# Attention and a gated long convolution on one core: the written order of all steps laid out anew, the last output rows staged in the buffers of k and v, the second sum on GpSimd in some batches

## The chip, the cores and the metric

The kernel runs on one core of a Trainium2 chip. The metric is the time of one execution on the device in microseconds (us). The engines are TensorE (PE; its weight loads are PEld), VectorE (DVE), ScalarE (ACT), GpSimd (POOL) and SyncE (SP). Each works through its own instructions in the order in which the program wrote them, and waits on semaphores for the others. SP, ACT and POOL also start transfers (DMAs).

## What is computed

Eight batches, each with 8 heads, 576 positions and 64 values a head. A linear attention without softmax is normalised and handed, as 576 x 512, to a gated convolution over the positions:

```python
def _attn_ref(q, k, v, g_norm):
    kv = np.einsum('bhsd,bhse->bhde', k, v)
    out = np.einsum('bhsd,bhde->bhse', q, kv)
    rms = np.sqrt(np.mean(out * out, axis=-1, keepdims=True) + 1e-06)
    return out / rms * g_norm
...
    x = attn_out.transpose(0, 2, 1, 3).reshape(B, S, H * D)
    proj = x @ w_proj
    x1, x2, x3 = proj[..., :D], proj[..., D:2 * D], proj[..., 2 * D:]
    X2 = np.fft.rfft(x2, n=S, axis=1)
    H = np.fft.rfft(filter_fft, n=S, axis=0)
    x2_conv = np.fft.irfft(X2 * H, n=S, axis=1)
    return (x1 * x2_conv * x3) @ w_out
```

Inputs and output are float32; products run in bfloat16.

## The kernel before, in words

The Fourier transforms are matmuls with tables of sines and cosines (IV, and FW, FX, FY, FT, FZ made from it by transposes), cut into three parts by folding the positions first (even and odd halves, then thirds). Everything is written as small steps, one function each in the dictionary `step`; the string `ORDER` names them one by one with their batch ("M0.3" is step M0 of batch 3), and a loop at the end calls them in that order. No scheduler moves anything: the string is the order of every engine's queue. A third number ("T0.0.18") puts so many idle matmuls (line 110, of zeros) in front of the step. PSUM is four pairs of banks; `take` hands a step the pair that has been free longest, and the step that evicts it calls `free`, so the order also decides who waits for whose eviction.

The steps of a batch, by engine:

- Loads on POOL's queue: Lk, Lv, Lq (a, b: half the heads), into two buffers each of k, v and q. Once at the start: the tables (Zi, Z, Zd, Zt, An, Zf, Tb0 to Tb2), the filter Lf with its products Ff (line 313) and H (lines 330, 333), and the weights Lw1 (first gate), Lw2 (x2), Lw3 (third), Lwo.
- q turned: T0, T1 on TensorE with the copies eTa, eTv (batches 0 and 1, line 413), Qt by transfers on SP, with a small copy on POOL that waits for it (line 401), from batch 2 on.
- K (line 375) multiplies k and v, eK (line 381) casts the product; O01 and O23 (line 440) multiply with q; sq (line 450, ACT) squares, R (line 447, PE) sums the squares, rs (line 461, ACT) takes the inverse root; ob (ACT, line 457) or ov (DVE, line 455) scales by g_norm; x0, x1 (DVE, line 475; two heads' pairs each) make x.
- eo, fr, fa (DVE, lines 487 to 498) fold x; rrM, rrT, abM, abT (PE, lines 515 to 535) multiply it with the middle third of w_proj; err, eab, eT (ACT, line 539) cast that; F0, F1t, F1, F2c, F2 (PE, lines 552 to 579) transform it.
- M0, M1 (DVE, line 587) multiply by the filter's spectrum into tpw, M2 (line 602) the third part; A0 and A1 are the sums of these products on POOL, Av0 and Av1 the same on DVE (all line 593). Before, A0 and Av1 are used in every batch.
- I01, I23, Io01, Io23 (PE, lines 641, 642) transform back, and need all sums; ea, oa (ACT, line 645) cast; vB, w, fin (DVE, lines 651 to 663) unfold and multiply with the gates' product, into yg.
- Ga0 to Ga3 and Gb0 to Gb3 (PE, line 612) are the gates, 8 matmuls each; x10 to x13 (ACT, line 618) cast the first, g0 to g3 (DVE, line 620) multiply the second with it.
- U0, U2, U4 (PE, lines 696, 709) multiply yg with w_out; ot0, ot2, ot4 (ACT) copy the result into one of five buffers ot and issue four transfers on SP (lines 700 to 716). For batch 7, V0 to V3 (line 732) take 128 rows each, va, vv copy them (ACT, DVE; line 737) into an ot too, and ds, dg, da (line 742) send them 32 rows at a time from SP, POOL or ACT.

The start (batch 0 up to K.1) and the end (from M0.7 on) are where one batch stands alone; in between, steps of up to four batches are mixed.

Of the kernel before, what the change touches and what calls it, by code (L numbers as in the profile page):

```python
# [23 lines left out]
ob1.1 Lk.2 err.0 sq0.1 abM.0 Gb2.0 ob0.1 F0.0 g2.0 eab.0 abT.0 eT.0 O23.1 F2c.0 F2.0 M0.0 sq2.1 ob2.1 Gb1.0 F1t.0 F1.0
M2.0 sq3.1 HN1.0 ob3.1 R1.1 g1.0 Lq.2 R0.1 Ga3.0 rs1.1 rs0.1 R2.1 K.2 Lq.3 A0.0 Qt.2 M1.0 R3.1 Qt.3 x13.0 rs2.1 x0.1
rs3.1 eK.2 Lk.3 Lv.3 Gb3.0 Av1.0 Io01.0 oa01.0 I01.0 x1.1 O01.2 Lwo.0 g3.0 ea01.0 Ga1.1 eo.1 sq1.2 Io23.0 ob1.2 R1.2
x11.1 Lv.4 Ga0.1 rs1.2 I23.0 oa23.0 fa.1 abM.1 sq0.2 fr.1 x10.1 ob0.2 ea23.0 vB.0 w.0 eab.1 abT.1 O23.2 rrM.1 eT.1
sq3.2 R0.2 rrT.1 ob3.2 rs0.2 fin.0 F2c.1 F2.1 err.1 Gb1.1 sq2.2 F0.1 M2.1 Ga3.1 ob2.2 Lk.4 g1.1 R3.2 Lq.5 x13.1 Lq.4
F1t.1 F1.1 rs3.2 M0.1 K.3 eK.3 R2.2 M1.1 Gb3.1 rs2.2 Gb0.1 g3.1 O23.3 U0.0 sq2.3 sq3.3 x1.2 g0.1 Ga2.1 Av1.1 x0.2 A0.1
ob3.3 ot0.0 Io01.1 x12.1 eo.2 oa01.1 fa.2 Gb2.1 I01.1 Io23.1 ob2.3 ea01.1 g2.1 Lv.5 abM.2 I23.1 oa23.1 abT.2 ea23.1  # L30
eab.2 eT.2 Ga0.2 x10.2 O01.3 K.4 Ga1.2 Qt.4 sq0.3 fr.2 ob0.3 eK.4 sq1.3 rrM.2 x11.2 F1t.2 F1.2 vB.1 w.1 rrT.2 R2.3
ob1.3 err.2 Gb0.2 rs2.3 fin.1 M1.2 F0.2 U2.0 R3.3 g0.2 rs3.3 Gb1.2 M0.2 F2c.2 F2.2 A0.2 ot2.0 g1.2 R0.3 M2.2 R1.3
Ga2.2 rs1.3 Ga3.2 x1.3 rs0.3 x0.3 x12.2 O23.4 Lq.6 x13.2 sq2.4 Av1.2 Gb2.2 ob2.4 U4.1 Lk.5 sq3.4 eo.3 ob3.4 g2.2 ot4.1
U0.1 fa.3 fr.3 Qt.5 R3.4 Io01.2 ot0.1 oa01.2 abT.3 rs3.4 I01.2 eT.3 ea01.2 Gb3.2 Io23.2 g3.2 oa23.2 I23.2 abM.3 ea23.2
eab.3 O01.4 rrM.3 F1t.3 F1.3 sq0.4 vB.2 w.2 ob0.4 sq1.4 rrT.3 err.3 M1.3 U2.1 ob1.4 F0.3 Ga1.3 R1.4 fin.2 ot2.1 x11.3
Ga0.3 Gb0.3 M0.3 R0.4 A0.3 rs1.4 x10.3 Av1.3 F2c.3 F2.3 Lv.6 rs0.4 g0.3 Gb1.3 R2.4 M2.3 rs2.4 g1.3 Lk.6 K.5 Io01.3
I01.3 x1.4 oa01.3 x0.4 eK.5 Ga2.3 x12.3 ea01.3 Ga3.3 O23.5 Io23.3 x13.3 oa23.3 sq3.5 ob3.5 U0.2 ot0.2 eo.4 I23.3 sq2.5
ob2.5 fa.4 Gb2.3 ea23.3 Lk.7 g2.3 abM.4 O01.5 fr.4 eab.4 abT.4 Gb3.3 Qt.6 sq0.5 eT.4 ob0.5 sq1.5 rrM.4 g3.3 R3.5 rrT.4
rs3.5 err.4 K.6 F1t.4 F1.4 eK.6 Ga1.4 ob1.5 R0.5 Ga0.4 x11.4 vB.3 w.3 F0.4 rs0.5 x10.4 fin.3 M1.4 M0.4 F2c.4 F2.4 R1.5
U2.2 rs1.5 Gb1.4 R2.5 M2.4 ot2.2 A0.4 g1.4 Ga3.4 O23.6 rs2.5 x13.4 sq2.6 x1.5 Av1.4 ob2.6 Gb0.4 sq3.6 Gb3.4 ob3.6 g0.4  # L40
g3.4 Ga2.4 x12.4 U4.3 x0.5 O01.6 Io01.4 eo.5 ot4.3 sq0.6 U0.3 oa01.4 ob0.6 fr.5 sq1.6 I01.4 Gb2.4 ob1.6 ea01.4 Lq.7
rrM.5 Io23.4 Lv.7 ot0.3 R0.6 g2.4 I23.4 rrT.5 oa23.4 rs0.6 K.7 fa.5 ea23.4 R1.6 abT.5 err.5 abM.5 rs1.6 vB.4 w.4 R3.6
Qt.7 eT.5 eK.7 eab.5 F0.5 Ga1.5 rs3.6 R2.6 F1t.5 F1.5 x11.5 fin.4 F2c.5 F2.5 rs2.6 M0.5 U2.3 M1.5 A0.5 ot2.3 Ga0.5
x10.5 M2.5 Gb1.5 x1.6 g1.5 Av1.5 O23.7 sq2.7 Gb0.5 Ga2.5 ob2.7 sq3.7 g0.5 Ga3.5 x0.6 x12.5 ob3.7 eo.6 I01.5 fa.6 Gb2.5
Io01.5 x13.5 g2.5 U0.4 Io23.5 oa01.5 Ga0.6 ea01.5 ot0.4 fr.6 oa23.5 I23.5 abM.6 ea23.5 abT.6 x10.6 Gb3.5 eab.6 O01.7
eT.6 Ga1.6 vB.5 w.5 g3.5 sq1.7 F1t.6 F1.6 ob1.7 fin.5 x11.6 sq0.7 rrM.6 R0.7 rrT.6 ob0.7 rs0.7 M1.6 F2c.6 F2.6 R1.7
err.6 M2.6 Gb0.6 rs1.7 F0.6 g0.6 U0.5 R2.7 M0.6 Ga2.6 x0.7 rs2.7 R3.7 x12.6 Gb1.6 Gb2.6 A0.6 ot0.5 rs3.7 Av1.6 g1.6
Ga3.6 g2.6 Io01.6 x1.7 eo.7 fr.7 I01.6 x13.6 Gb3.6 oa01.6 g3.6 Io23.6 ea01.6 U2.4 ot2.4 rrM.7 fa.7 Ga0.7 I23.6 oa23.6
# [4 lines left out]
dg13.7 V2.7 vv2.7 da20.7 dg21.7 ds22.7 da23.7 V3.7 va3.7 ds30.7 dg31.7 da32.7 ds33.7 ot2.6"""


@with_exitstack
def kernel(
# [402 lines left out]
    def e_rs(b, j):  # L460
        act.activation(out=halves(rstd()[:, j]), in_=tmp['r', b, j][:, :, 0:TH], func=AF.Abs_reciprocal_sqrt, scale=1.0 / D, bias=bias_eps)  # L461
# [151 lines left out]

    def gate_ev(b, dc, part):
        pp = tmp['g', b, dc, part]
        x1 = buf("x1", dc % 2, [P, 2, TH])
        if part == 0:
            act.copy(out=x1, in_=pp[:, :, 0:TH])  # L618
        else:
            vec.tensor_mul(out=halves(g13t()[:, dc]), in0=pp[:, :, 0:TH], in1=x1)  # L620
# [76 lines left out]

    def U_ev(b, c0):
        ot = ot_tile()
        act.copy(out=ot, in_=tmp['u', b, c0])  # L700
        free(("u", b, c0))
        for i in range(4):
            nc.sync.dma_start(out=o_rows(b, 2 * (b % 2) + 4 * c0 + i, 2 * (b % 2) + 4 * c0 + 4 + i), in_=ot[32 * i:32 * i + 32])
# [30 lines left out]
    def V_ev(b, key, ev):  # L734
        ot = tmp['ot', b, key] = ot_tile()
        k_ = ("u4", b) if key == 4 else ("v", b, key)
        ev(out=ot[:, 0], in_=tmp[k_])
        free(k_)

    def V_out(b, key, i, q):  # L740
        rows = o_rows(b - 1 + i // 2, (NB - 2, NB - 1, 0, 1)[i]) if key == 4 else o_rows(b, 2 * (b % 2) + 4 * key + i)
        q.dma_start(out=rows, in_=tmp['ot', b, key][32 * i:32 * i + 32, 0])
# [46 lines left out]
```

## Time and profile before

| | |
|---|---|
| runs | 225.63, 227.00, 227.52 us; median 227.0 |
| profiled execution | 227.53 us |
| its span | 225.8 us, 4943 instructions |
| busy: PE, DVE, ACT, POOL | 206.3, 174.9, 154.3, 51.1 us |
| mean granted clock of TensorE | 0.965 |
| read from and written to memory | 33.69 MB, 9.44 MB |

The span runs from the first instruction to the last on the core; the time of an execution also holds what lies around it. Durations in the text are of the profiled execution. A row of the timeline gives the start and the length in us, the engine, the line of the code, the operation, the tiles written and read, and behind them how long the engine had been idle and who ended that. PEq, SPq and the like are an engine's queue of transfers it issues; their length is the time until the last one was issued. The granted clock is 1.00 at full speed.

### The profile page before, as it was taken

Reading aid. Unit: us, or ns where it says so; the run is one execution under the profiler, and the core shown is the slowest. Engines: PE = TensorE matmul, PEld = TensorE weight load, DVE = VectorE, ACT = ScalarE, POOL = GpSimd, SP = SyncE. Lnnn points to the kernel's source line nnn. Section 1 sums busy time; section 2 is a strip of 40 time slices with the busy share of each in tenths; the row PEclk is TensorE's granted clock in tenths of the full one; section 3 lists DMA queues with packets and bytes.
Section 4 is the critical chain, followed back from the end, with each engine's and each line's share of the span. In section 5 each row is a group of like instructions: output and inputs, shape, how many; then the busy total and the mean of one; then the engine's idle time right before and its main releaser. Section 6 shows DMA issues by size and latency. Waiting matters only on the chain.

```text
span 225.8 us, 4943 instructions
## 1 busy us (share of the span) xinstructions
PE 206.3 (91%) x2025; PEld 119.4 (53%) x2025; DVE 174.9 (77%) x247; ACT 154.3 (68%) x245; POOL 51.1 (23%) x61
## 2 busy tenths in 40 slices
...
PEclk9985799999999999999999999999999999999995
...
GB/s 44 188 210 205 210 205 206 186 194 18 198 203 205 229 181 0 159 214 176 93 98 203 217 6 140 205 166 40 93 41 55 0 94 45 50 0 186 74 163 139
DMA packets 37049, 30.15 MB, mean 134 GB/s; under 512 B 16050, under 2 KB 32434, under 8 KB 37026
## 3 DMA queue, kind: packets, MB, share of 16 engines
...
q10 hardware_dynamic: 240, 0.33, 0.5%
q8 instruction: 16, 0.26, 0.5%
q14 instruction: 7, 0.06, 0.1%
HBM read 33.69 MB, written 9.44 MB: 191 GB/s over the span
## 4 chain that ended last, share of the span: by engine, by line
PE 63%; DVE 14%; ACT 9%; DMA 4%; POOL 4%; issue 2%; ACTq 1%; DVEq 0%; POOLq 0%
PE ps L612 20%; PE ps L696 9%; DVE tpw L587 5%; PE ps L529 5%; DMA vb<-in_v_dram 4%; PE ps L641 4%; PE ps L515 3%; PE ps L447 2%; PE ps L440 2%; PE ps L313 2%; PE ps L535 2%; PE ps L375 2%; POOL Y L593 2%; ACT ar L645 2%; PE ps L568 2%
## 5 line engine op out<-in xcount | busy, mean ns | idle before, releaser
L612 PE MATMUL ps<-x,wp 128*128 128x288 bf16 x512 | 70.8, 286 | 1.9 <-DVE Y L602 0.9
L612 PEld LDWEIGHTS <-wp 128*128 128x128 bf16 x512 | 48.9, 97 | 19.4 <-issue 4.5
L593 POOL TENSOR_TENSOR Y<-tpw 97x1024 bf16<-97x1024 f32 x8 | 21.4, 2669 | 73.2 <-DVE tpw L587 73.2
L587 DVE TENSOR_TENSOR tpw<-ps,HH 97x2048 f32<-97x2048 f32 (+1 forms) x16 | 36.3, 2284 | 0.6 <-PE ps L568 0.6
L620 DVE TENSOR_TENSOR g<-ps,x 128x576 bf16<-128x576 f32 x32 | 24.1, 754 | 15.0 <-PE ps L612 12.5
L461 ACT ACTIVATE rstd<-ps,bias_eps 128x576 bf16<-128x576 f32 x32 | 23.4, 746 | 9.8 <-PE ps L447 9.6
L618 ACT CAST x<-ps 128x576 bf16<-128x576 f32 x32 | 20.5, 640 | 9.2 <-PE ps L612 5.8
L696 PE MATMUL ps<-wo,yg 128*128 128x512 bf16 x112 | 26.3, 379 | 0.5 <-DVE tpw L587 0.4
L700 ACT COPY ot<-ps 128x1024 f32<-128x1024 f32 x14 | 14.2, 1017 | 14.3 <-PE ps L696 13.7
L645 ACT CAST ar<-ps 128x576 bf16<-128x576 f32 x32 | 19.8, 646 | 5.8 <-PE ps L642 5.6
L539 ACT CAST x<-ps 128x1024 bf16<-128x1024 f32 (+1 forms) x24 | 20.8, 879 | 2.9 <-PE ps L529 2.2
L450 ACT ACTIVATE sq<-ps 128x576 bf16<-128x576 f32 x32 | 20.8, 660 | 2.8 <-PE ps L440 2.0
L457 ACT ACTIVATE o<-ps,g_col 128x576 bf16<-128x576 f32 x28 | 21.1, 755 | 0.0
L696 PEld LDWEIGHTS <-yg 128*128 128x128 bf16 x112 | 10.6, 97 | 12.8 <-issue 1.3
L641 PE MATMUL ps<-IV,Y 128*128 128x192 bf16 x128 | 16.7, 246 | 0.6 <-DVE Y L593 0.4
L401 POOL COPY one__101<-qT 1x2 bf16<-1x2 bf16 x6 | 1.7, 286 | 62.3 <-DMA qT<-qb 62.3
L529 PE MATMUL ps<-wp,ab 128*128 128x512 bf16 x64 | 15.2, 380 | 0.5 <-DVE ab L491 0.5
L447 PE MATMUL ps<-sq,ind 128*128 128x288 bf16 x64 | 13.6, 305 | 0.6 <-ACT rstd L461 0.6
L642 PE MATMUL ps<-IV,Y 97*128 97x96 bf16 x64 | 13.3, 208 | 0.2 <-POOL Y L593 0.2
L651 DVE TENSOR_TENSOR vt<-ar 128x768 bf16<-128x768 bf16 (+1 forms) x9 | 4.6, 512 | 11.4 <-ACT ar L645 11.4
L475 DVE TENSOR_TENSOR x<-o,rstd 128x1152 bf16<-128x1152 bf16 x16 | 12.3, 780 | 0.5 <-ACT rstd L461 0.5
L641 PEld LDWEIGHTS <-Y 128*128 128x128 bf16 x128 | 10.2, 98 | 3.6 <-DVE Y L593 0.9
(139 smaller groups left out, 310.3 us busy)
## 6 DMA issues: line engine op xcount, KB each, us to landing
...
kb<-in_k_dram POOLq DMA_DIRECT2D x7, 576.0 KB, 12.1
vb<-in_v_dram POOLq DMA_DIRECT2D x7, 576.0 KB, 12.6
wp<-in_moe_w_proj_dram POOLq DMA_DIRECT2D x3, 512.0 KB, 17.0
out_dram<-ot SPq DMA_DIRECT2D x20, 64.0 KB, 2.5
...
```

What stands on the lines that cost most here:

```text
L450: act.activation(out=halves(sq()[:, j]), in_=tmp['o', b, j][:, :, 0:TH], func=AF.Square)
L457: act.activation(out=halves(osb()[:, j]), in_=i_, func=AF.Copy, scale=g_col)
L461: act.activation(out=halves(rstd()[:, j]), in_=tmp['r', b, j][:, :, 0:TH], func=AF.Abs_reciprocal_sqrt, scale=1.0 / D, bias=bias_eps)
L529: nc.tensor.matmul(pp[:, h], abt()[:, j, 2 * h * P:(2 * h + 1) * P], w2(j), start=(j == 0), stop=(j == NDC - 1))
L539: act.copy(out=o_(), in_=tmp[key, b])
L587: vec.tensor_mul(out=t_[:n], in0=xp[:n].unsqueeze(1).to_broadcast([n, 2, 2, DM]), in1=two)
L593: op(out=Yt()[:n, 2 * g:2 * g + 2], in0=t_[:n, ::-1, 0], in1=t_[:n, ::-1, 1])
L612: nc.tensor.matmul(pp[:, h, 0:TH], w_, x[:, j, h * TH:(h + 1) * TH], start=(j == 0), stop=(j == NDC - 1))
L620: vec.tensor_mul(out=halves(g13t()[:, dc]), in0=pp[:, :, 0:TH], in1=x1)
L641: nc.tensor.matmul(pp[:, i, 0:SB], Y[:, 2 * g + h, cs], IV[:, 2 * g + h, 0:SB], start=(g == 1), stop=(g == 2))
L645: ev(out=art()[:, d0:d0 + 2, h], in_=tmp['i', b, d0, h][:, :, 0:TH])
L696: nc.tensor.matmul(pp[:, cc], ygt(b)[:, dc, b % 2 * 64 + c * P:b % 2 * 64 + (c + 1) * P], wo[:, dc], start=(dc == 0), stop=(dc == NDC - 1))
```

## The change

It replaces `ORDER` as a whole and adds steps that the new order uses. Nothing of the arithmetic changes. In words:

- The start: q, v and k of batch 0 are loaded in interleaved halves (Lqa, Lva, Lka, Lvb, Lkb, Lqb); the products and O01 of the first half come before those of the second; idle matmuls stand in seven places (20, 5, 3, 1, 4, 2, 3: 38) where there were two (18, 2: 20); the load of ScalarE's table (Act) comes after the first squares. In later batches q or k is loaded as halves in some cases.
- A1 (POOL) stands in place of Av1 (DVE) in batches 1 and 3 to 7, Av0 (DVE) in place of A0 (POOL) in 4, 5 and 6.
- Some evictions change engine: eTa (the q copy) goes from DVE to ACT, the casts eK of the first half to DVE, err of batch 0, three of x1 and three of oa, ea to DVE. Some steps of DVE come as halves, and x in batches 1, 6 and 7 as a whole.
- The copies of the last 128-row pieces (V_ev) go into the k and v buffers, seen as float32, and that of U4.7 into sq; U2.6's copy goes to DVE (ov2r), ahead of the last one; the transfers of these rows are issued from POOL, ACT and SP.
- All long-lived tiles are made before the loop.

Cut to its core:

```diff
-ORDER = """Lq.0 Z.0 Zi.0 Lkb.0 Lka.0 Zd.0 Zt.0 Lva.0 An.0 Lvb.0 Zf.0 T0.0.18 Act.0 Tb0.0 Lf.0 eTv0.0 Lw1.0 Tb2.0 Tb1.0 Ka.0 eKa.0
+ORDER = """Lqa.0 Zi.0 Lva.0 Zd.0 Z.0 T0.0.20 Lka.0 Lvb.0 Zt.0 Lkb.0 An.0 Lqb.0 Zf.0 eTa0.0 Tb2.0.5 Ka.0 eKva.0 Tb0.0 O01.0.3
...
+    vec3 = (vec.tensor_copy,) * 3
...
+        step["eKv" + n_] = lambda b, j0=j0: kv_ev(b, j0, j0 + 2, vec3)
+        step["eKa" + n_] = lambda b, j0=j0: kv_ev(b, j0, j0 + 2, act3)
...
-        step["eTa%d" % jj] = lambda b, jj=jj: q_ev(b, jj, (vec.tensor_copy, vec.tensor_copy)[jj])
+        step["eTa%d" % jj] = lambda b, jj=jj: q_ev(b, jj, act.copy)
...
+        def fv(b):
+            vec.tensor_copy(out=o_(), in_=tmp[key, b])
+            free((key, b))
+        step["v" + name] = fv
...
+        step["xv%d" % dc] = lambda b, dc=dc: gate_ev(b, dc, 0, vec.tensor_copy)
...
+        step["ov%dr" % c0] = lambda b, c0=c0: U_ev(b, c0, vec.tensor_copy)
...
     def V_ev(b, key, ev):
-        ot = tmp['ot', b, key] = ot_tile()
+        st = sq() if key == 4 else kvq["kkvv"[key]][key % 2]
+        ot = tmp['ot', b, key] = st.rearrange("p a b -> p (a b)" if key == 4 else "p j c d -> p (j c d)").bitcast(FP32)[:, 0:DM]
...
+    for t in (sq, osb, rstd, eot, abt, rrt, g13t, yg4, art, bbt, wt):
+        t()
```

ScalarE's queue at the start, from the last tables on (IV) up to the first rstd, before. L240 is the table load, L281 to L280 the table copies, L381 the casts of the k and v products, L450 the squares:

```order
L240 ACT_TABLE_LOAD
L281 COPY FW<-ps_67 128x768
L279 COPY FY<-ps_68 128x128
L280 COPY FZ<-ps_68 128x64
L281 COPY FW<-ps_68 32x768
L381 CAST kvblk_78<-ps_67 64x2x64 x2
L381 CAST kvblk_78<-ps_66 64x2x64 x2
L450 ACTIVATE sq<-ps_67 128x576
L450 ACTIVATE sq<-ps_69 128x576
L450 ACTIVATE sq<-ps_68 128x576
L450 ACTIVATE sq<-ps_66 128x576
L461 ACTIVATE rstd<-ps_67,bias_eps 128x576
```

And now, with the lines of the changed file (L420 is the q copy, L283 the table copies, L457 the squares, L464 the scaled o, L242 the table load, L383 the casts, L468 the rstd):

```order
L420 COPY qT<-ps_66 128x1152
L281 COPY FY<-ps_67 128x128
L282 COPY FZ<-ps_67 128x64
L283 COPY FW<-ps_67 32x768
L283 COPY FW<-ps_69 128x768
L457 ACTIVATE sq<-ps_67 128x576
L457 ACTIVATE sq<-ps_66 128x576
L464 ACTIVATE o<-ps_67,g_col 128x576
L242 ACT_TABLE_LOAD
L383 CAST kvblk_78<-ps_69 128x2x64
L383 CAST kvblk_78<-ps_69 64x2x64 x2
L468 ACTIVATE rstd<-ps_66,bias_eps 128x576
```

The q copy and a scaled o have come in, and the table load and the second half's casts stand behind the first two squares.

VectorE's queue from fin.6 to the first step after the inverse transforms of batch 7, before (tpw are the products M0 and M1, g the gates' products, Y the third part and the second sum):

```order
L663 TENSOR_TENSOR yg<-w,g_483 128x4x576
L587 TENSOR_TENSOR tpw<-ps_66,HH 97x2048
L620 TENSOR_TENSOR g_483<-ps_69,x_452 128x576
L602 TENSOR_TENSOR Y<-ps_67,HM 128x1024
L587 TENSOR_TENSOR tpw<-ps_66,HH 128x2048
L593 TENSOR_TENSOR Y<-tpw 128x1024
L620 TENSOR_TENSOR g_483<-ps_68,x_608 128x576
L651 TENSOR_TENSOR vt<-ar 128x384
```

And now:

```order
L683 TENSOR_TENSOR yg<-w,g_108 128x4x576
L606 TENSOR_TENSOR tpw<-ps_67,HH 97x2048
L606 TENSOR_TENSOR tpw<-ps_69,HH 128x2048
L621 TENSOR_TENSOR Y<-ps_68,HM 128x1024
L639 TENSOR_TENSOR g_108<-ps_69,x_115 128x576
L639 TENSOR_TENSOR g_108<-ps_68,x_118 128x576
L665 CAST ar<-ps_69 128x2x288
L671 TENSOR_TENSOR vt<-ar 128x384
```

M1.7 has moved up to M0.7, the sum has left, and an inverse transform's cast has come in. On GpSimd the last sums were these, ahead of the transfers:

```order
L138 DMA qb_75<-in_q_dram 96x8x384
L142 DMA vb_73<-in_v_dram 128x4x576
L401 COPY one__101<-qT 1x2
L593 TENSOR_TENSOR Y<-tpw 97x1024 x3
L742 DMA out_dram<-ot 32x512 x7
```

And now (128x1024 is the second sum, 97x1024 the first):

```order
L140 DMA qb_75<-in_q_dram 96x4x384
L144 DMA vb_73<-in_v_dram 128x4x576
L612 TENSOR_TENSOR Y<-tpw 128x1024
L408 COPY one__101<-qT 1x2
L612 TENSOR_TENSOR Y<-tpw 128x1024 x2
L612 TENSOR_TENSOR Y<-tpw 97x1024
L612 TENSOR_TENSOR Y<-tpw 128x1024
```

GpSimd makes A1.4 to A1.6 and, for batch 7, A0 and then A1; the copy that waits for q of batch 7 stands between.

ScalarE's queue at the end, from the copy of U4.5 on, before:

```order
L713 COPY ot<-ps_67 128x512
L737 COPY ot<-ps_68 128x512
L742 DMA out_dram<-ot 32x512 x2
L737 COPY ot<-ps_67 128x512
L742 DMA out_dram<-ot 32x512 x2
L737 COPY ot<-ps_66 128x512
L742 DMA out_dram<-ot 32x512
L700 COPY ot<-ps_69 128x1024
```

And now (L733 is U4.5's copy, L760 those of the last pieces, L765 their transfers):

```order
L733 COPY ot<-ps_67 128x512
L760 COPY sq<-ps_66 128x512
L760 COPY kb_70<-ps_66 128x512
L765 DMA out_dram<-kb_70 32x512
L760 COPY vb_73<-ps_69 128x512
L765 DMA out_dram<-kb_70 32x512
L765 DMA out_dram<-vb_73 32x512
L765 DMA out_dram<-kb_70 32x512
L765 DMA out_dram<-vb_73 32x512
L760 COPY vb_72<-ps_69 128x512
L765 DMA out_dram<-vb_72 32x512 x2
L765 DMA out_dram<-kb_71 32x512 x2
```

The copies write sq, k and v instead of ot, U2.6's copy (L700 before) is gone from this queue, and nine transfers stand between and behind the copies where there were five.

More of the change, by code (lines that the diff above doesn't have):

```diff
@@ L24 @@
[L24 to L48, printed above, removed]
```

70 lines of the change are left out of this document (54 added, 16 removed).

## Prediction

> **What bounds the kernel now.** I read the page first, then the busy times by stretch, the timeline of both ends, the groups by form for prices, and the rows of the tile tpw for the sums. The profiled execution took 227.53 us for a span of 225.8, so 1.73 lie around the span; the median of the runs is 227.0, 0.5 under it.
>
> ```profile
> span 225.8 us, 4943 instructions
> ...
> PEclk9985799999999999999999999999999999999995
> ```
>
> ```profile
> 8.00:16.00 8.00, 4.85 (x123) 3.46 (x123) 4.30 (x25) 5.89 (x12) 4.10 (x6) 0.97 1.18 212
> 16.00:26.00 10.00, 9.38 (x62) 3.07 (x61) 7.68 (x12) 6.52 (x11) 1.61 (x3) 0.51 1.23 202
> 26.00:40.00 14.00, 14.00 (x175) 7.41 (x174) 8.80 (x16) 9.10 (x15) 0.77 (x1) 1.00 1.23 208
> 40.00:80.00 40.00, 37.50 (x425) 22.98 (x424) 33.73 (x38) 33.39 (x57) 11.75 (x12) 1.00 1.05 178
> 80.00:200.00 120.00, 118.28 (x1134) 71.32 (x1126) 101.84 (x113) 87.99 (x139) 21.39 (x17) 1.00 0.55 105
> ...
> 210.00:217.40 7.40, 6.40 (x29) 2.56 (x28) 4.00 (x9) 1.76 (x3) 2.38 (x5) 1.00 0.45 111
> 217.40:225.80 8.40, 0.00 (x0) 0.00 (x0) 0.00 (x0) 1.60 (x2) 1.14 (x3) 0.67 0.58 154
> ```
>
> The columns behind the length are PE, PEld, DVE, ACT and POOL busy, then the granted clock. From 80 to 200 us TensorE is busy 118.28 of 120 at full clock: no order makes that stretch shorter by more than 1.7 us, while a worse one can lengthen it. From 40 to 80 another 2.5 us are idle. What an order can win lies at the ends: 3.15 idle in 8 to 16, ten microseconds at half clock (0.51) in 16 to 26, 1.0 idle in 210 to 217.4, and 8.40 us after the last matmul.
>
> **The change, part one: the start.** These rows are the anchors of before: the end of the tables (ACT, 8.97 + 1.38 = 10.35), the last half of v, O23.0, x1.0, K.1, and rrT.0.
>
> ```profile
> 8.97 1.38 ACT L236 ACTIVATE IV<-ang,cosb 128x576 bf16<-128x576 f32 x2
> ...
> 10.37 1.28 ACT L240 ACT_TABLE_LOAD   x1
> ...
> 14.55 0.48 PE L375 MATMUL ps<-vb,kb 64*64 64x64 bf16 x36 [0.80 <-DMA vb<-in_v_dram]
> ...
> 17.59 0.70 PE L440 MATMUL ps<-qT,kvblk 64*64 64x288 bf16 x8
> ...
> 23.14 0.75 DVE L475 TENSOR_TENSOR x<-o,rstd 128x1152 bf16<-128x1152 bf16 x1
> ...
> 35.40 0.78 PE L375 MATMUL ps<-vb,kb 64*64 64x64 bf16 x72
> ...
> 38.48 0.62 PE L522 MATMUL ps<-wp,rr 128*64 128x512 bf16 x4
> ```
>
> And these are the prices, by form (busy us, mean ns of one, idle before):
>
> ```profile
> L620 DVE TENSOR_TENSOR g<-ps,x 128x576 bf16<-128x576 f32 x32 | 24.1, 754 | 15.0 <-PE ps L612 12.5 <-ACT ar L645 1.8 <-ACT rstd L461 0.2
> L461 ACT ACTIVATE rstd<-ps,bias_eps 128x576 bf16<-128x576 f32 x32 | 23.4, 746 | 9.8 <-PE ps L447 9.6
> ...
> L457 ACT ACTIVATE o<-ps,g_col 128x576 bf16<-128x576 f32 x28 | 21.1, 755 | 0.0
> L450 ACT ACTIVATE sq<-ps 128x576 bf16<-128x576 f32 x32 | 20.8, 660 | 2.8 <-PE ps L440 2.0 <-DVE g L620 0.8
> ...
> L413 DVE COPY qT<-ps 128x1152 bf16<-128x1152 bf16 x4 | 3.0, 750 | 0.2 <-PE ps L409 0.2
> ...
> L315 ACT CAST ff<-ps 128x1024 bf16<-128x1024 f32 x2 | 2.0, 1012 | 3.0 <-PE ps L313 3.0
> ...
> L346 DVE SCALAR_TENSOR_TENSOR HH<-ps,cf,hu 128x512 f32<-128x512 f32 x2 | 1.4, 748 | 0.1
> ...
> L491 DVE TENSOR_TENSOR ab<-eo 128x768 bf16<-128x768 bf16 x2 | 1.1, 554 | 0.0
> ...
> L381 ACT CAST kvblk<-ps 64x128 bf16<-64x128 f32 x4 | 1.0, 260 | 2.1 <-DVE kvblk L381 2.0
> ...
> L281 ACT COPY FW<-ps 128x768 bf16<-128x768 bf16 x1 | 0.8, 799 | 0.0
> ```
>
> Loads come as halves and q, k, v interleaved, so half the heads are ready earlier, and 18 more idle matmuls stand on TensorE between the first products. They cost nothing where TensorE would wait anyway (3.15 us idle in 8 to 16). But the new order gives ScalarE more to do before the first x, and it does it in a row. From 10.35: the q copy of 1152 columns (no ACT row; between 0.80 for 768 columns and 0.80 x 1152/768 = 1.20, I take 1.15) to 11.5; the Tb2 copies, 0.5 of small ones (bounded by 0.26 for the small kvblk cast) and 0.80, to 12.8; FW 0.80, 13.6; two squares 1.32, 14.9; o 0.75, 15.7; the table load 1.28, which now stands behind them, 17.0; three casts eKab 0.8, 17.8. So O23.0 starts near 17.9, as before (17.59). Then two rstd 1.5, two squares and an o 2.1, two ff 2.0, two rstd 1.5: 24.9, and x1.0 on VectorE ends near 25.7, later than before (23.89). Behind it stand on VectorE the qT copy 0.75, six scalar_tensor_tensor 4.5, the second eo (0.9, two passes below the 0.55 of ab each), fr and fa at some 1.1 each and g1.0 0.75, which frees the PSUM of K.1: 25.7 + 9.1 = 34.8 without further waits, and I allow 0.5: K.1 at 35.3, the time of before (35.40). But by then rrM.0 and rrT.0 and as many gates as before plus one are done. Before, that state is reached at 38.48 + 0.62 = 39.1, less what it has done that the new order has not (K.1 0.78 and O01.1 0.4): 37.9. The start gives 37.9 - 35.3 = -2.6. Bounds: 0, if what is early here waits again in the 2.5 idle us of 40 to 80, and -4.6, half of the 9.38 us at half clock, if those come back whole.
>
> The clock decides that range. Before, with TensorE busy 4.85 of 8, it fell to 0.51 for ten microseconds; the new row of idle matmuls fills much of 8 to 18, but between the filter products and the H products TensorE waits for the ff and rstd of ScalarE, some 2 us by the walk above. [...]
>
> **Part two: the second sum.** The rows of the tile tpw give least, median and greatest duration in ns of GpSimd's and of VectorE's sum; the timeline behind them shows a place where GpSimd's sum ran beside VectorE's work on SBUF:
>
> ```profile
> L593 POOL TENSOR_TENSOR Y<-tpw x8: 2355/2360/3931, 45.1 to 198.9; 97x1024 bf16<-97x1024 f32 x8
> L593 DVE TENSOR_TENSOR Y<-tpw x8: 1214/1218/1226, 50.0 to 202.8; 128x1024 bf16<-128x1024 f32 x8
> ```
>
> ```profile
> 180.64 0.75 DVE L475 TENSOR_TENSOR x<-o,rstd 128x1152 bf16<-128x1152 bf16 x1
> 180.81 3.93 POOL L593 TENSOR_TENSOR Y<-tpw 97x1024 bf16<-97x1024 f32 x1 [22.60 <-DVE tpw L587]
> ...
> 181.31 1.22 DVE L593 TENSOR_TENSOR Y<-tpw 128x1024 bf16<-128x1024 f32 x1
> ...
> 184.24 1.12 DVE L475 TENSOR_TENSOR x<-o,rstd 128x1152 bf16<-128x1152 bf16 x1
> ```
>
> Six sums move to GpSimd (batches 1, 3 to 7) and three of the first kind move to VectorE (4 to 6): VectorE gets 5 instead of 8 (-3.7 us), GpSimd 11 instead of 8 (+7.1). The sum at 180.81 took 3.93 instead of 2.36: it got through only once VectorE's x and second sum had ended (182.53 + 2.3 = 184.8). If every microsecond of GpSimd's sums stopped VectorE, VectorE would be 7.1 - 3.7 = 3.4 us worse; if none, 3.7 better. VectorE has 18 us free between 80 and 200, so I take 0 for TensorE, with -0.5 and +3.4 as ends. [...] Behind M1.7, GpSimd's two sums follow each other, 2 x 2.36 from the end of M0.7, while TensorE has U0.6, U2.5, Gb0.7 and Gb3.7: about even, cost 0.
>
> The other splits of VectorE's steps and the evictions that move from ScalarE to VectorE cost VectorE a few us, hidden by the same 18. SP and POOL issue more, smaller loads; no row shows TensorE waiting for a load after 14.55, so 0.
>
> **Part three: the end.**
>
> ```profile
> 214.64 2.75 PE L732 MATMUL ps<-wo,yg 128*128 128x512 bf16 x12
> 215.07 6.12 SPq L742 DMA_DIRECT2D out_dram<-ot  x8
> ...
> 216.56 0.69 DVE L737 COPY ot<-ps 128x512 f32<-128x512 f32 x1 [2.40 <-PE ps L732]
> 216.57 1.47 POOL L742 DMA_DIRECT2D out_dram<-ot  x3 [1.47 <-ACT ot L737]
> ...
> 218.28 0.58 ACT L737 COPY ot<-ps 128x512 f32<-128x512 f32 x1 [1.99 <-DMA out_dram<-ot]
> ...
> 219.33 1.01 ACT L700 COPY ot<-ps 128x1024 f32<-128x1024 f32 x1 [0.47 <-ACT ot L737]
> ...
> 221.28 1.82 SPq L703 DMA_DIRECT2D out_dram<-ot  x4
> ```
>
> ```profile
> out_dram<-ot POOLq DMA_DIRECT2D x7, 64.0 KB, 2.1
> ```
>
> The last matmul ends at 217.39. The last-but-one copy waits 1.99 us for a free ot, the copy of U2.6 stands behind it, and its four transfers stand behind eight others on SP: 8.4 us. With k, v and sq as buffers that wait goes, and U2.6 is followed by V2 and V1 on TensorE, eight matmuls at 2.75/12 = 1.8 us, which hide its copy on VectorE (the nearest row, 1.22 for 1024 columns of another step). What remains behind the last matmul: 0.2 to the copy, 0.69, two issues on GpSimd at 1.47/3 (1.0), 2.1 to landing, and 0.4 as between landing and the end before: 4.4. That is -4.0. Behind M0.7 the new order keeps six gates for TensorE where before four were left, so of the 1.0 idle in 210 to 217.4 I take half: -0.5. Together -4.5. Bounds: -1.5, if ScalarE's nine transfers, which stand between its copies, wait as SP's eight did (6.12 against 8 x 0.46 = 3.7), and -5.
>
> Sum: -2.6 + 0 - 4.5 = -7.1; 227.53 - 7.1 = 220.4.
>
> **Rivals.** First, the clock falls again at the start, while TensorE waits for ScalarE near 21 to 24 us, and H and gates run at half speed as the ten microseconds did before: the start gives 0, 227.5 - 4.5 = 223. For it: ScalarE's unbroken chain; against it: the idle matmuls. Second, the end is bound by the queues of ScalarE: -2.6 - 1.5, 223.4; for it SP's 6.12, against it three queues. Third, the other sign: the inverse transforms wait for the second sum. [...] For it: only 1.7 us of 120 are idle, so nothing in the middle absorbs a late sum; against it: gates stand between sum and transform. Fourth, the clock stays full, the start gives -4.6, and half of the 2.5 idle us of 40 to 80 goes with it: 227.5 - 4.6 - 1.2 - 4.5 = 217.2. [...]
>
> **How the numbers follow.** Forecast 0.43, its own range 218 to 222.7; clock lost 0.19; queues 0.06; late sums 0.17; full clock 0.10; port 0.05. A measurement of this kernel tells about 1% (2.3 us) from nothing. Faster by more: 0.43, 0.10 and 0.17 of the three cases near 223.5, which lie at the edge, 0.70; within: the other 0.13 of those; slower: the late sums, 0.17. The range goes from 216, a little below the full clock, to 228, which leaves out the late sums and little else.
>
> **What would show it.** Right: clock at 1.0 between 16 and 26, K.1 near 35.3 with rrT.0 ahead of it, no wait of ScalarE for out_dram, 4 to 5 us behind the last matmul. Wrong: TensorE's weight loads waiting for POOL Y in total by more than 5 us, or 80 to 200 stretched; then the third rival holds.

## The result, and the profile after

| | before | after |
|---|---|---|
| median of the runs | 226.3 us (4 runs, 225.5 to 227.5) | 235.2 us (4 runs, 234.5 to 235.3) |
| profiled execution, its span | 227.5, 225.8 us | 234.5, 232.7 us |
| last matmul ends, span behind it | 217.4, 8.4 us | 224.4, 8.3 us |

The ratio is 1.038 [1.032, 1.044]: 8.9 us slower, where 7 us faster was forecast. An execution that took over 1.5% longer than the fastest of its kernel is left out of the medians below. The page of the profile after has the place of the loss already. Each slice is 5.8 us: TensorE (row PE) is almost idle in the two from 46.5 to 58 us, and the granted clock is below full speed in the two from 52 to 64.

```profile
span 232.7 us, 5024 instructions
...
PE   7999989910999899989979999999989999999850
...
PEclk9999999995799999999999999999999999999996
```

The busy times by stretch of the profile after, with the same columns as in the prediction (PE, PEld, DVE, ACT, POOL busy, clock, share of the DMA engines, GB/s):

```profile
8.00:16.00 8.00, 7.96 (x136) 4.35 (x135) 4.07 (x23) 7.61 (x13) 4.72 (x7) 1.00 1.19 203
16.00:26.00 10.00, 9.62 (x103) 4.79 (x101) 5.99 (x9) 9.54 (x15) 2.27 (x3) 1.00 1.23 202
26.00:40.00 14.00, 13.38 (x158) 7.17 (x156) 12.27 (x17) 8.71 (x15) 2.26 (x3) 1.00 1.24 206
40.00:60.00 20.00, 8.97 (x139) 5.93 (x138) 9.98 (x10) 8.48 (x16) 4.22 (x5) 0.78 1.11 162
60.00:80.00 20.00, 18.62 (x205) 10.82 (x204) 16.16 (x16) 16.40 (x28) 7.40 (x7) 0.96 0.75 120
80.00:200.00 120.00, 116.49 (x1140) 71.86 (x1137) 111.24 (x144) 87.99 (x136) 24.85 (x21) 1.00 0.62 117
...
224.39:232.70 8.31, 0.00 (x0) 0.00 (x0) 0.69 (x1) 0.58 (x1) 2.94 (x6) 0.77 0.68 174
```

Up to 40 us the clock is as forecast, 1.00 where it had been 0.51. From 80 to 200 TensorE is busy 1.8 us less than before. But from 40 to 60 TensorE is busy 8.97 of 20, ScalarE 8.48, while the DMA engines are busier than before (1.11 against 0.87); before, TensorE had 18.90 and ScalarE 18.81:

```profile
40.00:60.00 20.00, 18.90 (x214) 11.39 (x213) 15.27 (x17) 18.81 (x33) 8.62 (x10) 1.00 0.87 142
```

The waits of TensorE name who ended them (what waited, whom for: us in total, times, the longest):

```profile
PE ps L662 <- POOL Y L612: 11.0, 1, 11.0
PE ps L631 <- DVE g L639: 1.9, 2, 1.0
```

One wait of 11.0 us, for a sum on GpSimd. To see why the sum was late, follow it backwards in the timeline of the kernel after:

```profile
37.78 2.29 DVE L606 TENSOR_TENSOR tpw<-ps,HH 97x2048 f32<-97x2048 f32 x1 [0.69 <-DMA qb<-in_q_dram]
38.84 19.09 SPq L407 DMA_TRANSPOSE qT<-qb  x2
...
55.78 0.17 POOL L408 COPY one__101<-qT 1x2 bf16<-1x2 bf16 x1 [18.72 <-DMA qT<-qb]
55.92 2.33 POOL L612 TENSOR_TENSOR Y<-tpw 97x1024 bf16<-97x1024 f32 x1
...
58.31 0.26 PE L662 MATMUL ps<-IV,Y 97*128 97x96 bf16 x1 [11.02 <-POOL Y L612]
```

The products that the sum reads were there at 40.07. GpSimd was idle, 18.72 us in one piece up to 55.78. It stood at the small copy that belongs to Qt.2 and waits for the turned q of batch 2, and A0.0, the first sum of batch 0, is written behind Qt.2. That transfer took 16.8 us; the rows of the tile qT have the others:

```profile
DMA to landing us min/median/max: 4.7/5.0/16.8
```

Before, the transfers took 5.2 to 8.3, and the sum ran ahead of the copies:

```profile
DMA to landing us min/median/max: 5.2/6.3/8.3
```

```profile
45.07 2.36 POOL L593 TENSOR_TENSOR Y<-tpw 97x1024 bf16<-97x1024 f32 x1 [13.70 <-DVE tpw L587]
...
48.96 0.17 POOL L401 COPY one__101<-qT 1x2 bf16<-1x2 bf16 x1 [1.53 <-DMA qT<-qb]
```

The end after, answering to the rows of part three of the prediction:

```profile
222.50 1.89 PE L754 MATMUL ps<-wo,yg 128*128 128x512 bf16 x8
...
223.56 0.58 ACT L760 COPY vb<-ps 128x512 f32<-128x512 f32 x1 [2.87 <-PE ps L754]
...
223.95 4.59 SPq L723 DMA_DIRECT2D out_dram<-ot  x4
...
225.66 0.58 ACT L760 COPY vb<-ps 128x512 f32<-128x512 f32 x1 [1.51 <-DMA out_dram<-kb]
...
227.50 0.98 POOL L765 DMA_DIRECT2D out_dram<-kb  x2
```

The wait for a free ot is gone, but a copy waits for a transfer again (1.51), SP takes 4.59 us for four issues, and the end stands 8.3 us behind the last matmul (222.50 + 1.89 = 224.4), not 4.4.

### The profile page after: what moved, and what is told of

Same layout as the page of the kernel before. It is cut to its first block, busy times and chain, and to the rows that moved or that the text cites. A ratio compares the mean times of both kernels' runs of the same rounds, so it can differ in the third digit from the quotient of the medians.

```text
span 232.7 us, 5024 instructions
## 1 busy us (share of the span) xinstructions
PE 205.1 (88%) x2043; PEld 121.2 (52%) x2043; DVE 184.7 (79%) x271; ACT 152.3 (65%) x238; POOL 61.6 (26%) x72
## 4 chain that ended last, share of the span: by engine, by line
PE 65%; DVE 15%; DMA 7%; ACT 5%; issue 3%; POOL 2%; ACTq 1%; POOLq 0%; DVEq 0%
PE ps L631 19%; DMA qT<-qb 7%; PE ps L716 7%; PE ps L543 6%; PE ps L661 5%; DVE tpw L606 4%; PE ps L112 4%; DVE g L639 3%; PE ps L549 3%; DVE Y L612 2%; PE ps L529 2%; PE ps L447 2%; DVE x L489 2%; PE ps L454 2%; PE ps L377 2%
## 5 line engine op out<-in xcount | busy, mean ns | idle before, releaser
L612 POOL TENSOR_TENSOR Y<-tpw 128x1024 bf16<-128x1024 f32 (+1 forms) x11 | 27.0, 2459 | 92.1 <-DVE tpw L606 92.1
L468 ACT ACTIVATE rstd<-ps,bias_eps 128x576 bf16<-128x576 f32 x32 | 23.5, 749 | 7.1 <-PE ps L454 7.0
L665 ACT CAST ar<-ps 128x576 bf16<-128x576 f32 x29 | 17.8, 645 | 15.8 <-PE ps L662 15.4
L637 ACT CAST x<-ps 128x576 bf16<-128x576 f32 x29 | 18.6, 643 | 9.7 <-PE ps L631 9.6
L553 ACT CAST x<-ps 128x1024 bf16<-128x1024 f32 (+1 forms) x23 | 19.6, 872 | 6.1 <-PE ps L543 2.4
L457 ACT ACTIVATE sq<-ps 128x576 bf16<-128x576 f32 x32 | 20.4, 656 | 3.0 <-PE ps L447 2.8
L464 ACT ACTIVATE o<-ps,g_col 128x576 bf16<-128x576 f32 x28 | 20.5, 751 | 2.5 <-DVE x L489 2.5
L720 ACT COPY ot<-ps 128x1024 f32<-128x1024 f32 x13 | 13.1, 1015 | 10.3 <-PE ps L716 10.3
L716 PEld LDWEIGHTS <-yg 128*128 128x128 bf16 x112 | 10.5, 98 | 11.7 <-issue 0.7
L489 DVE TENSOR_TENSOR x<-o,rstd 128x1152 bf16<-128x1152 bf16 (+1 forms) x13 | 13.2, 1031 | 2.2 <-ACT rstd L468 2.1
L671 DVE TENSOR_TENSOR vt<-ar 128x384 bf16<-128x384 bf16 (+1 forms) x11 | 4.9, 443 | 12.1 <-ACT ar L665 12.0
L112 PE MATMUL ps<-nil,ind 128*128 128x512 bf16 x38 | 12.0, 463 | 1.7 <-DVE ind L193 1.6
L621 DVE TENSOR_TENSOR Y<-ps,HM 128x1024 bf16<-128x1024 f32 x8 | 9.8, 1219 | 4.1 <-PE ps L598 2.9
L454 PE MATMUL ps<-sq,ind 128*128 128x288 bf16 x64 | 12.7, 286 | 0.4 <-ACT ff L317 0.4
```

Source lines behind the costliest of these rows:

```text
L112: nc.tensor.matmul(pair[i][:, j], ind, nil, start=True, stop=True)
L457: act.activation(out=halves(sq()[:, j]), in_=tmp['o', b, j][:, :, 0:TH], func=AF.Square)
L464: act.activation(out=halves(osb()[:, j]), in_=i_, func=AF.Copy, scale=g_col)
L553: act.copy(out=o_(), in_=tmp[key, b])
L612: op(out=Yt()[:n, 2 * g:2 * g + 2], in0=t_[:n, ::-1, 0], in1=t_[:n, ::-1, 1])
L716: nc.tensor.matmul(pp[:, cc], ygt(b)[:, dc, b % 2 * 64 + c * P:b % 2 * 64 + (c + 1) * P], wo[:, dc], start=(dc == 0), stop=(dc == NDC - 1))
```

## The experiments

**Theory Q** (queue): A0.0 stands behind Qt.2 on GpSimd; ahead of it, it costs nothing. **Theory T** (transfer): the turned q itself is late, because loads are issued ahead of it; then TensorE waits for q once it no longer waits for the sum. The first runs edit the order in either way and in both, and move the sum alone in the kernel before.

The sum ahead (e1):

```diff
-Ga2.0 Qt.2 rs2.1 x12.0 R1.1 K.2 A0.0 M1.0
+Ga2.0 A0.0 Qt.2 rs2.1 x12.0 R1.1 K.2 M1.0
```

> The changed kernel with one word moved: A0.0 stands ahead of Qt.2 on GpSimd. Theory Q (the 11 us of TensorE waiting for the first sum of batch 0 are GpSimd's queue alone: the sum stands behind a copy that waits for the transfer that turns q of batch 2): the sum runs at 40 to 42.5 us, the wait goes, 11 us come back and the clock does not fall: 222 to 224. Rival T (the transfer that turns q is itself late, and TensorE needs its result at O01.2, right behind the inverse transforms): the sum runs early all the same, but O01.2 waits for qT until 55 to 56 us, only 1.5 to 4 us come back: 231 to 233.5.

Measured 231.95 us, 1.028 [1.025, 1.031]. From its timeline, GpSimd's sum and the matmuls with the turned q:

```profile
40.46 2.36 POOL L612 TENSOR_TENSOR Y<-tpw 97x1024 bf16<-97x1024 f32 x1 [3.10 <-DVE tpw L606]
...
55.66 0.69 PE L447 MATMUL ps<-qT,kvblk 64*64 64x288 bf16 x8 [6.81 <-DMA qT<-qb]
```

The sum is out of the way, and TensorE waits 6.81 us for q itself. Only 3.2 of the 8.9 us come back by the medians, 2.1 by the spans of the profiled executions (232.7 and 230.6). Theory T holds for this run.

The loads behind (e2):

```diff
-F1.0 Lv.3 R3.1 R2.1 Lq.3 ob2.1 rs3.1 Ga2.0 Qt.2 rs2.1
+F1.0 R3.1 R2.1 ob2.1 rs3.1 Ga2.0 Qt.2 Lv.3 Lq.3 rs2.1
```

> The changed kernel with two words moved: the loads Lv.3 and Lq.3 stand behind Qt.2 on GpSimd, so they are not in flight beside the transfer that turns q; the sum A0.0 stays behind. Theory Q: the sum still stands behind the copy; it starts when the transfer lands, and if that is still late nothing changes: 234 to 235. Rival T (the transfer took 16.8 us from issue to landing because loads of v and q of batch 3 run beside it): it lands 8 us earlier, near 47 to 48, the sum ends near 50, TensorE waits 2 to 4 us instead of 11: 226 to 229.

Measured 233.59 (3 runs), 1.036 [1.032, 1.041]. GpSimd's copies and sum, and TensorE behind them:

```profile
48.98 0.58 POOL L408 COPY one__101<-qT 1x2 bf16<-1x2 bf16 x1 [21.56 <-DMA qT<-qb]
51.06 2.35 POOL L612 TENSOR_TENSOR Y<-tpw 97x1024 bf16<-97x1024 f32 x1
53.47 0.26 PE L662 MATMUL ps<-IV,Y 97*128 97x96 bf16 x1 [5.96 <-POOL Y L612]
...
72.42 0.36 POOL L408 COPY one__101<-qT 1x2 bf16<-1x2 bf16 x1 [16.03 <-DMA qT<-qb]
...
78.32 0.50 PE L661 MATMUL ps<-IV,Y 128*128 128x192 bf16 x2 [2.76 <-POOL Y L612]
```

The turned q lands near 49 instead of 55.8, so the two loads ahead of it account for some 7 us; it still takes 9.9 us from its issue at 39.04, and what holds it for the rest was not tried. TensorE still waits 5.96 us for the sum behind it, and the loads that were pushed back make q of batch 3 late (72.42). So the transfer moved as theory T says, but the time did not fall to the 226 to 229 that it forecast.

Both (e3):

> The changed kernel with both moves. Theory Q: as with the first move alone, 222 to 224. Rival T: both are needed, only here the whole wait goes: 221 to 224, and at least 5 us below each move alone.

Measured 234.33, 1.039 [1.034, 1.044]: as slow as the change itself. The rows of TensorE that read the turned q of batches 2 and 3:

```profile
48.64 0.44 PE L447 MATMUL ps<-qT,kvblk 64*64 64x288 bf16 x8 [0.16 <-DMA qT<-qb]
```

```profile
73.49 0.69 PE L447 MATMUL ps<-qT,kvblk 64*64 64x288 bf16 x8 [5.32 <-DMA qT<-qb]
```

At batch 2 nothing waits any more (0.16), and the wait stands one batch later, 5.32 us, behind Lq.3. Neither theory had said that: each had looked at one batch. q of each batch has to be loaded, turned, and turned in time, and in this order q of 3 is loaded too late. From 60 to 80 us TensorE is busy 13.10 us, at a mean clock of 0.74:

```profile
60.00:80.00 20.00, 13.10 (x137) 7.06 (x138) 9.61 (x11) 6.60 (x11) 6.11 (x5) 0.74 0.82 126
```

That is how one wait of 5.32 us, and one of 2.46 for VectorE's products near 60, can cost as much as the 11.0 of the change. The waits are not all of the loss, for the matmuls behind them are slow: eight of line 631 took 1.93 us at 64.04, behind the wait of 2.46, and 2.02 at 77.51, behind that of 5.32, against 1.14 at 45.83; the mean granted clock is 0.83 from 60 to 70 us and 0.66 from 70 to 80.

The kernel before, with its sum behind both copies (e4):

```diff
-R2.1 K.2 Lq.3 A0.0 Qt.2 M1.0 R3.1 Qt.3 x13.0
+R2.1 K.2 Lq.3 Qt.2 M1.0 R3.1 Qt.3 A0.0 x13.0
```

> The kernel before with one word moved: A0.0 behind Qt.2 and Qt.3 on GpSimd. Theory Q: the sum moves from 45.1 to about 54 us (the second copy ran at 53.1), the first inverse transform of batch 0, at 51.4, waits for it until 56.4, TensorE loses 4 to 5 us: 230 to 232. Rival T: TensorE would have to wait for qT soon anyway: 227 to 228.5.

Measured 232.92, 1.031 [1.028, 1.035]: 7 us from one word, 0.9 above the range of theory Q. The sum and the transform that needs it:

```profile
52.33 2.33 POOL L593 TENSOR_TENSOR Y<-tpw 97x1024 bf16<-97x1024 f32 x1
...
54.71 0.26 PE L642 MATMUL ps<-IV,Y 97*128 97x96 bf16 x1 [5.66 <-POOL Y L593]
```

Theory Q holds by itself in the old order: the place of one sum behind copies that wait is enough. The wait is 5.66 of the 7 us. The mean granted clock is 0.66 from 50 to 60 us, where it was 1.00 before, and two matmuls of line 641 took 0.52 us right behind the wait and 0.33 at 58.19.

The change with both faults mended for both batches (g1): Lq.3 comes early, the sum stands ahead of Qt.2, and the other loads behind it. Lk.3 and Qt.3 leave their old places further back, which the cut does not show.

```diff
-Lv.2 sq3.1 Lwo.0 F2c.0 ... Lv.3 R3.1 R2.1 Lq.3 ob2.1 rs3.1 Ga2.0 Qt.2 rs2.1 x12.0 R1.1 K.2 A0.0 M1.0
+Lv.2 Lq.3 sq3.1 F2c.0 ... R3.1 R2.1 ob2.1 rs3.1 Ga2.0 A0.0 Qt.2 Lv.3 Lk.3 Qt.3 Lwo.0 rs2.1 x12.0 R1.1 K.2 M1.0
```

> The changed kernel with GpSimd's queue of the first 40 us laid out for the turned q: Lq.3 follows Lv.2, A0.0 stands ahead of Qt.2, and behind Qt.2 come Lv.3, Lk.3, Qt.3 and Lwo.0. Theory (the 12 us lost in the middle are q of batches 2 and 3 being turned late, beside loads, with the first sum queued behind): both transfers land before TensorE needs them, no wait over 1 us for qT or for GpSimd's first sum before 80 us: 219 to 222. Rival (the later shares of the new order, sums on GpSimd and splits, cost as much by themselves): TensorE finds other waits in 60 to 80, 224 to 229.

Measured 223.57 (10 runs), 0.990 [0.986, 0.993]: 11.6 us below the change and 1% below before, 1.6 above the range that was expected. The longest wait of this kind that is left:

```profile
50.01 0.44 PE L447 MATMUL ps<-qT,kvblk 64*64 64x288 bf16 x8 [1.40 <-DMA qT<-qb]
```

So the loss of the change lies in the order of loads, turned q and sum between 35 and 75 us: mending that alone gives back more than the 8.9 us. What the rest of the change is worth can't be read from g1 alone, since its loads stand in another order than those of before too. The next kernels vary g1.

The sums on the engines of before (g2): A0 on GpSimd and Av1 on VectorE in all batches.

```diff
-A1.1 A1.3 ... A1.7 Av0.4 Av0.5 Av0.6
+Av1.1 Av1.3 ... Av1.7 A0.4 A0.5 A0.6
```

> The same as g1_turned_q_early, and the two sums on the engines of before in every batch: first on GpSimd, second on VectorE. [...] Rival (the sums on GpSimd take load from VectorE): 1 to 4 us slower than g1.

Measured 225.79 (8 runs), 1.000 [0.995, 1.004], 2.2 us above g1 by the medians and 1.0 by the spans of the profiled executions (222.8 and 221.8). The rival holds: 2.2 us lie in its 1 to 4. The busy times from 60 to 80 us, of g2 and of g1:

```profile
60.00:80.00 20.00, 17.30 (x278) 11.28 (x276) 18.13 (x23) 13.51 (x23) 5.95 (x6) 1.00 1.03 178
```

```profile
60.00:80.00 20.00, 18.69 (x283) 11.95 (x282) 19.25 (x24) 14.98 (x25) 7.36 (x7) 1.00 1.03 180
```

The sums as the change has them help: in g1 TensorE is busy 1.4 us more in that stretch. Among the waits of TensorE in g2 are 3.1 us for VectorE's sums, which g1 doesn't have.

The copy of V2 ahead of eight transfers, of which ScalarE issues four (g3):

```diff
-va3.7 da03.7 da31.7 da01.7 ds43.7 dg30.7 ds40.7 dg32.7 da33.7 va2.7
+va3.7 va2.7 da03.7 da31.7 da01.7 ds43.7 dg30.7 ds40.7 dg32.7 da33.7
```

> The same as g1_turned_q_early, and ScalarE's copy va2 directly behind va3, ahead of the four transfers that ScalarE issues between them. Theory (ScalarE's transfers hold up its last copy, and what GpSimd sends behind it): the copy runs 1.5 us earlier and the end comes 1 to 1.5 us earlier than in g1. Rival (the last transfers of SP, behind VectorE's copy of U2.6, end last anyway): within 0.4 us of g1.

Measured 223.47, 0.991 [0.989, 0.994]: nothing gained. The copy moved to 213.31, the end did not.

The idle matmuls of before (g4): 18 and 2 in their two places instead of 38 in seven.

> The same as g1_turned_q_early, with the idle matmuls of before (18 and 2 instead of 38 in seven places). Theory C (they keep TensorE's clock up at the start): the granted clock falls to half for some microseconds between 14 and 30 us, and the time is 1.5 to 4 us above g1. Rival (the new order keeps TensorE busy enough by itself, or ScalarE is the bound there): within 0.7 us of g1.

Measured 223.72, 0.993 [0.991, 0.994]: as g1. The clock's row changes, the time does not; of g4, at the start:

```profile
8.00:16.00 8.00, 4.99 (x124) 3.37 (x121) 4.64 (x24) 7.94 (x14) 4.73 (x7) 1.00 1.18 202
16.00:26.00 10.00, 10.00 (x89) 4.24 (x87) 5.34 (x8) 9.24 (x14) 2.28 (x3) 0.83 1.24 203
```

ScalarE is busy 7.94 of 8 and 9.24 of 10 there, and TensorE runs at a mean clock of 0.83 from 16 to 26 us with the time that g1 has at 1.00.

The end, by three theories, is told by the gap: the time from the end of the last matmul to the end of the span. **Copies** (the prediction's): the wait for a free ot binds. **Bytes**: the 1.3 to 1.4 MB still to be written behind the last matmul bind (154 GB/s for 8.4 us before, 174 for 8.3 after); this was read from g1, where the DMA engines have a share of 0.82 to 0.99 from 214 to 220. **Count**: the number of transfers binds, since issues and copies wait for the landing of others. First the buffers alone, in the kernel before (h3), and the last 512 KB written earlier, in g1 (h1):

```diff
-        ot = tmp['ot', b, key] = ot_tile()
+        st = sq() if key == 4 else kvq["kkvv"[key]][key % 2]
```

> The kernel before with one edit: the copies of the last pieces go into the buffers of k, v and sq, its written order unchanged. That takes away ScalarE's wait of 1.99 us for a free ot and nothing else; before ends 8.4 us behind its last matmul. The prediction's step (the wait for ot and the queues behind it bind the end): 1.5 to 2 us faster, ratio near 0.992. Theory bytes: some 1.3 MB are still to be written behind the last matmul at 154 to 200 GB/s, the copies of V3 and U2.6 come 2 us earlier but their rows stand behind the others': 0 to 0.8 us faster, ratio 0.997 to 1.

Measured 225.87 (12 runs), 0.999 [0.995, 1.003]. Without the wait for ot the end stands 8.5 us behind the last matmul, as before. The theory of the copies falls: the wait for a free ot does not bind.

```diff
-U4.5 x12.7 ot4.5 ... V3.7 dg42.7 U2.6 dg00.7 ... da22.7 ov2r.6 da20.7
+U4.5 U2.6 x12.7 ot4.5 ot2.6 ... V3.7 dg42.7 dg00.7 ... da22.7 da20.7
```

> The turned-q order (g1) with U2.6, the last 512 KB piece, right behind U4.5 and its copy on ScalarE behind that of U4.5, instead of third from the end. In g1 the last matmul ends at 213.4 and the span at 221.8; its transfers run at a share of 0.8 to 1.0 from 214 to 220, but at 0 from 206 to 208 and 0.18 from 212 to 214. Theory bytes (what binds the end is the 2 MB still to be written from 207 on, some 200 GB/s): with the 512 KB sent from about 209 on, the last matmul stays near 213.4 and the end comes 1.5 to 3.5 us earlier: 220 to 222 against 223.6, gap behind the last matmul 5 to 7 us. Rival queues (the end is bound by copy, issue and one landing behind the last matmul, and by the waits of the queues): no gain, 223 to 224.5, since the last three copies stand where they stood. Second rival: TensorE waits for f001 and f023 with U2.6 gone from behind them, and the last matmul is 1 to 2 us later: 223 to 224.

Measured 223.38, 0.986 [0.980, 0.992], no different from g1; 8.0 us behind the last matmul. SP's four transfers of U2.6 were issued over 5.68 us, and those behind them came last:

```profile
210.91 5.68 SPq L723 DMA_DIRECT2D out_dram<-ot  x4
218.81 0.80 SPq L765 DMA_DIRECT2D out_dram<-sq  x2
```

The bytes did not leave earlier, so this run doesn't decide. Two kernels come nearer to it. l1 sends the first half of each of the last five pieces' rows, half the bytes in as many transfers; l2 sends every second of their transfers at full width, ten in place of twenty. Both leave half of these output values out.

```diff
-        q.dma_start(out=rows, in_=tmp['ot', b, key][32 * i:32 * i + 32])
+        q.dma_start(out=rows[:, 0:DM // 2], in_=tmp['ot', b, key][32 * i:32 * i + 32, 0:DM // 2])
```

> The turned-q order (g1), in which each of the twenty transfers of the last five pieces (V_out) sends 256 of 512 columns; half of those output values are left out. Same number of transfers, same issues and waits, 0.64 MB less. In g1 the end comes 8.4 us behind the last matmul. Theory bytes (at 200 to 225 GB/s behind the last matmul, of which 0.4 MB fall away): gap 6 to 7 us, time 221.5 to 222.3 against 223.6. Theory count (what binds is that each of many transfers is issued behind the landing of an earlier one, whatever its size): gap 8 to 8.5 us, 223 to 224.

```diff
+        if i % 2 == 0:
-        q.dma_start(out=rows, in_=tmp['ot', b, key][32 * i:32 * i + 32])
+            q.dma_start(out=rows, in_=tmp['ot', b, key][32 * i:32 * i + 32])
```

> The turned-q order (g1), in which only ten of the twenty transfers of the last five pieces (V_out, the first and third 32 rows of each) are sent, at full width; half of those output rows are left out. The same 0.64 MB less, half the transfers, half the issues. Theory bytes: as with half rows, gap 6 to 7 us, 221.5 to 222.3. Theory count: the gap falls by far more than with half rows, to 5 to 6 us, 220.5 to 221.5, and half rows does not move.

Measured 223.73 (9 runs, 222.6 to 225.4), 0.993 [0.988, 0.997], and 223.16 (4 runs), 0.988 [0.984, 0.992]. The two times are too near each other to decide. In the profiled executions the last matmul of l2 came 1.9 us later than that of l1; l2's mean granted clock was 0.96 from 40 to 80 us, where l1 has 1.00, a stretch that the edit at the end does not touch. The last steps stand alike against the last matmul (the copy of U2.6 starts 1.7 us ahead of its end in g1 and in l2), so the gaps can be compared, of g1, of l1 and of l2:

```profile
213.53:221.80 8.27, 0.00 (x1) 0.00 (x0) 0.69 (x1) 0.58 (x1) 2.94 (x6) 0.82 0.69 174
```

```profile
213.77:221.90 8.13, 0.00 (x0) 0.00 (x0) 0.69 (x1) 0.58 (x1) 2.94 (x6) 0.69 0.49 121
```

```profile
215.62:222.30 6.68, 0.00 (x1) 0.00 (x0) 0.69 (x1) 0.25 (x1) 0.98 (x2) 0.73 0.55 137
```

Half the bytes change 8.27 to 8.13, and the share of the DMA engines falls from 0.69 to 0.49: they were not the bound. Half the transfers, with the same bytes as l1, bring 6.68, not down to the 5 to 6 expected. Each gap is of one execution; those of before, after, h1 and h3, with all of the transfers, lie between 8.0 and 8.5. The theory of the bytes falls, and that of the count holds in kind; how the count makes the time is read only from waits. In l1 SP still waits for a landing:

```profile
SPq L723 <- DMA out_dram<-kb: 2.5, 1, 2.5
```

The times from issue to landing show how little the bytes matter there. GpSimd's of v and k, in g1 and in l1 (KB each, median us):

```profile
out_dram<-vb POOLq DMA_DIRECT2D x4, 64.0 KB, 2.7
out_dram<-kb POOLq DMA_DIRECT2D x3, 64.0 KB, 2.8
```

```profile
out_dram<-vb POOLq DMA_DIRECT2D x4, 32.0 KB, 2.2
out_dram<-kb POOLq DMA_DIRECT2D x3, 32.0 KB, 2.7
```

Half the size saves 0.5 and 0.1 us. In both most of the time is left, 2.2 of 2.7 and 2.7 of 2.8. Why an issue waits for the landing of a transfer from another buffer was not tried.

## Why the prediction was wrong

The step that failed is this one of part two: "SP and POOL issue more, smaller loads; no row shows TensorE waiting for a load after 14.55, so 0." Between K.1 and the last matmul it cost most of 10.5 us (last matmul 224.4 - 217.4 = +7.0, on top of a start that is 3.5 us earlier), 18.90 - 8.97 = 9.9 of it between 40 and 60. The row was right, and the conclusion was not, for it shows the waits of the old order. Qt.2 had been moved ahead of A0.0 in GpSimd's queue, with Lv.3 and Lq.3 ahead of both, and that queue was not walked at this place, only at the end. In place of 0 the runs show 11.0 us of waiting for a sum that stands behind the turned q, and, with the sum out of the way, 6.81 for the turned q itself. Every instruction that a step issues counts, its small copy too: the row of 48.96 above, 1.53 us of wait behind the sum, is the one that would have asked the question.

Point by point:

- **The start**, forecast -2.6: K.1 came at 34.44 (forecast 35.3), the same work stood at 37.9 before, so -3.5, within the bounds. The walk was pessimistic by 0.9 (x1.0 ended at 24.75, not 25.7):

```profile
23.99 0.76 DVE L489 TENSOR_TENSOR x<-o,rstd 128x1152 bf16<-128x1152 bf16 x1 [0.89 <-ACT rstd L468]
...
34.44 0.78 PE L377 MATMUL ps<-vb,kb 64*64 64x64 bf16 x72 [0.62 <-DVE g L639]
```

But most of it is the half clock of the profiled execution of before, and not every execution has that. In the profile of h3, whose order is that of before, the clock is 1.00 from 16 to 26 and rrT.0 comes at 35.88 instead of 38.48. The runs of before fall into two groups, which fits this: of 17 in one round, eight had a mean clock of 0.958 to 0.966 and took 226.6 to 227.6 us, nine had 0.975 to 0.989 and took 225.0 to 225.8. The two rows of h3:

```profile
16.00:26.00 10.00, 8.27 (x90) 4.51 (x91) 9.06 (x17) 7.96 (x13) 1.56 (x3) 1.00 1.25 204
```

```profile
35.88 0.62 PE L522 MATMUL ps<-wp,rr 128*64 128x512 bf16 x4
```

Against such an execution the new start wins 3.5 - 2.6 = 0.9 us. That is one reason why g1 gains 1% and not 7 us. The first rival (clock falls again) did not come, nor did the fourth's 217.2. What lets the clock fall in one execution of an order and not in another was not shown.

- **The second sums**, forecast 0 with -0.5 and +3.4 as ends: mis-sized. By g2 against g1, with the order mended, they bring a gain of 1.0 (spans) to 2.2 us (medians), outside these ends. Behind M1.7 it was about even, as forecast: no wait of TensorE for the two sums of batch 7. The third rival has the right sign and not the right cause: no transform waits for a second sum, one waits for a first. What was to show it, TensorE waiting for POOL's Y by more than 5 us in total, did come, with 11.0; it was drawn too wide to tell the two sums apart.

- **Sums beside each other**, the 0.05 for a port: no run shows a port, nor that every microsecond of GpSimd's sums stops VectorE. In its place the runs show sums that get longer beside each other, at a small price. Two that ran on both engines at once (1.22 and 2.36 alone) in the timeline after:

```profile
97.48 2.35 POOL L612 TENSOR_TENSOR Y<-tpw 97x1024 bf16<-97x1024 f32 x1 [6.36 <-DVE tpw L606]
97.91 3.00 DVE L612 TENSOR_TENSOR Y<-tpw 128x1024 bf16<-128x1024 f32 x1
```

Such collisions are two (the other is GpSimd's sum at 166.06, 3.40 us, beside VectorE's at 167.83, 2.71), and TensorE's whole loss from 80 to 200 us is 1.8. What makes them longer was not shown.

- **The end**, forecast -4.5: 8.3 us behind the last matmul against 8.4, so -0.1. This term failed too. The walk counted one copy, two issues and one landing, and left out that the queues wait for landings: in the profile after SP waits 2.9 us for one ahead of an issue for U2.6, and ScalarE the 1.51 above. The second rival (1.5) was nearer; its cause, waits of the queues, fits l1 and l2, though it is not ScalarE's alone.
